# Interleaving attention and MoE by half sequence, with paired heads in row and column tiles

## The chip, the cores and the metric

The kernel runs on one core of one Trainium2 chip. A core has TensorE (matrix products), VectorE, ScalarE (functions by table), GpSimd and SyncE, which all run their own instruction streams, and 16 DMA engines that they share. The metric is the device time of one execution in microseconds. Runs of a kernel are marked fast or slow; slow means over 1.5% above the fastest run of the same kernel. Only fast runs are compared, except where the text says otherwise.

## The reference

```python
# q, k, v: (4 batches, 8 heads, 768 positions, 64), inputs about 0.1 in size
scores = q @ k.T / 8                       # per batch and head
causal = i >= j
stream = causal & ((j < 4) | (i - j < 64)) # 4 sink keys, window of 64
mask = causal for heads 0, 2, 6 ; stream for heads 1, 3, 4, 5, 7
attn = softmax(where(mask, scores, -1e9)) @ v
x = attn as (3072 tokens, 512)             # head h gives columns 64h..64h+63
h = x @ w_in                               # (512, 2048)
g = h * sigmoid(beta * h)                  # a beta for each of the 2048
out = g @ w_out                            # (2048, 512)
```

Three heads ("retrieval") attend to everything before them, five ("streaming") to four sink keys and the last 64 positions. The kernels leave the maximum out of the softmax, which these small scores permit.

## The kernel before

It works in three stages: load and rescale the weights, attention of all batches and heads, then the MoE layer. Matrix operands are bf16, and every exponential is taken with keys on the partitions and queries along the columns.

```python
# stage 1: weights arrive in fp32 and are rescaled by VectorE, so that one
# table function serves: beta*h = x @ (w_in*beta), g = silu(beta*h)/beta
nc.vector.tensor_mul(w_in_sb[:, mo, :], w_in_f[:, mo, :], beta_bc)      # 4 x
...
# stage 2: for 16 pairs (batch, two neighbouring heads)
def part1(b, hp):
    # 6 loads by SyncE in fp32, 3 VectorE copies to bf16 (V with a column of ones)
    ...
    for t in range(T):                       # T = 6 blocks of 128 positions
        nc.tensor.transpose(tpq, q2b[:, t, :, :], ident_bf)
        nc.any.tensor_copy(out=QT2[:, t * 128:(t + 1) * 128], in_=tpq)
        ...                                  # the same for k
    for hh in range(2):
        for idx, (kj, ca, cb) in enumerate(plan):  # key block kj, query blocks ca..cb
            nc.tensor.matmul(sp[:, 0:w], KT2[po:po + D, kj * 128:(kj + 1) * 128],
                             QT2[po:po + D, ca * 128:(cb + 1) * 128], ...)
            nc.scalar.activation(out=esd, in_=sp[:, 0:w], func=Exp, scale=scale)
            ...                              # product with an fp32 mask by VectorE
def part2(st):
    for hh in range(2):
        for qi in range(T):
            for j, (idx, kj, cc) in enumerate(contrib):
                nc.tensor.matmul(pout, es_all[:, hh, idx, cc*128:(cc+1)*128],
                                 V_ext[:, kj, hh, :], ...)       # 65 columns
            nc.vector.reciprocal(rec, pout[:, D:D + 1])
            nc.vector.tensor_scalar(out=oqd2[:, qi, hh, :], in0=pout[:, 0:D],
                                    scalar1=rec, ..., op0=mult)
    ...                                      # 6 transposes back, copied into xT
# stage 3: for 6 chunks of 512 tokens
for fi in range(FO):                         # 16 blocks of 128 hidden units
    ...                                      # 4 matmuls of 512 columns into hp_
    nc.scalar.activation(out=gT[:, fi, :], in_=hp_, func=Silu)
for ns in range(4):
    ...                                      # 16 matmuls of 512 columns into op
    nc.scalar.copy(out=osb, in_=op)          # and a store
```

A streaming head takes the first key block against all queries (for the sinks) and each other key block against two query blocks. That makes 768 + 4 x 256 + 128 = 1920 score columns for 768 queries, and most query blocks sum over three value matmuls.

The softmax here doesn't subtract the row's maximum and nothing guards it: scores larger than these inputs give would overflow.

Of the kernel before, what the change touches and what calls it, by code (L numbers as in the profile page):

```python
# [8 lines left out]
F32 = mybir.dt.float32  # L9
BF16 = mybir.dt.bfloat16  # L10
GE = mybir.AluOpType.is_ge


def _aff(nc, buf, cm, fstep, base, n):
    nc.gpsimd.affine_select(
        out=buf,
        in_=buf,
        compare_op=GE,
        fill=0.0,
        base=base,  # L20
        pattern=[[fstep, n]],
        channel_multiplier=cm,
    )


@with_exitstack
def kernel(
# [16 lines left out]
    d_model = moe_w_in.shape[0]  # L44
    d_ff = moe_w_in.shape[1]
    N = B * S
    MO = d_model // 128
    FO = d_ff // 128
    NCHUNK = 512
    NCH = N // NCHUNK  # L50

    retr = [1, 0, 1, 0, 0, 0, 1, 0]
    n_sink_i = 4
    window_i = 64
    scale = 1.0 / (D ** 0.5)

    consts = ctx.enter_context(tc.tile_pool(name="consts", bufs=1))

    def new_mask(nm):
        m = consts.tile([128, 128], F32, name=nm)  # L60
        nc.gpsimd.memset(m, 1.0)
        return m

    Mc = new_mask("Mc")
    _aff(nc, Mc, -1, 1, 0, 128)
    Msd = new_mask("Msd")
    _aff(nc, Msd, -1, 1, 0, 128)
    _aff(nc, Msd, 1, -1, window_i - 1, 128)
    Mso = new_mask("Mso")
    _aff(nc, Mso, 1, -1, -(128 - window_i + 1), 128)  # L70
    Msink = consts.tile([128, 128], F32, name="Msink")
    nc.gpsimd.memset(Msink, 0.0)
    nc.gpsimd.memset(Msink[0:n_sink_i, :], 1.0)
    Msink_c = consts.tile([128, 128], F32, name="Msink_c")
    nc.gpsimd.memset(Msink_c, 0.0)
    nc.gpsimd.memset(Msink_c[0:n_sink_i, :], 1.0)
    _aff(nc, Msink_c, -1, 1, 0, 128)
    Mso_sink = consts.tile([128, 128], F32, name="Mso_sink")
    nc.vector.tensor_max(Mso_sink, Mso, Msink)
    M00s = consts.tile([128, 128], F32, name="M00s")  # L80
    nc.vector.tensor_max(M00s, Msd, Msink_c)

    ident_f32 = consts.tile([128, 128], F32, name="idf")
    make_identity(nc, ident_f32)
    ident_bf = consts.tile([128, 128], BF16, name="idb")
    nc.vector.tensor_copy(out=ident_bf, in_=ident_f32)

    Mstr0 = consts.tile([128, T * 128], F32, name="Mstr0")
    nc.vector.tensor_copy(out=Mstr0[:, 0:128], in_=M00s)
    nc.vector.tensor_copy(out=Mstr0[:, 128:256], in_=Mso_sink)  # L90
    for t in range(2, T):
        nc.vector.tensor_copy(out=Mstr0[:, t * 128:(t + 1) * 128], in_=Msink)
    Mstrd = consts.tile([128, 256], F32, name="Mstrd")
    nc.vector.tensor_copy(out=Mstrd[:, 0:128], in_=Msd)
    nc.vector.tensor_copy(out=Mstrd[:, 128:256], in_=Mso)

    big = ctx.enter_context(tc.tile_pool(name="big", bufs=1))
    xT = big.tile([128, MO, N], BF16)
    w_in_sb = big.tile([128, MO, d_ff], BF16)
    w_out_sb = big.tile([128, FO, d_model], BF16)  # L100

    with tc.tile_pool(name="wstage", bufs=1) as wstage:
        beta_row = wstage.tile([1, d_ff], F32)
        nc.sync.dma_start(out=beta_row, in_=moe_beta.rearrange("(o f) -> o f", o=1))
        beta_bc = wstage.tile([128, d_ff], F32)
        nc.gpsimd.partition_broadcast(beta_bc, beta_row)  # L106
        beta_p = wstage.tile([128, FO], F32)
        nc.sync.dma_start(out=beta_p, in_=moe_beta.rearrange("(fo fi) -> fi fo", fi=128))
        invb = wstage.tile([128, FO], F32)
        nc.vector.reciprocal(invb, beta_p)  # L110

        w_in_f = wstage.tile([128, MO, d_ff], F32)
        nc.sync.dma_start(
            out=w_in_f,
            in_=moe_w_in.rearrange("(mo mi) f -> mi mo f", mi=128),
        )
        for mo in range(MO):
            nc.vector.tensor_mul(w_in_sb[:, mo, :], w_in_f[:, mo, :], beta_bc)  # L118

        w_out_f = wstage.tile([128, FO, d_model], F32)  # L120
        nc.sync.dma_start(
            out=w_out_f,
            in_=moe_w_out.rearrange("(fo fi) d -> fi fo d", fi=128),
        )
        for fo in range(FO):
            nc.vector.tensor_scalar(  # L126
                out=w_out_sb[:, fo, :],
                in0=w_out_f[:, fo, :],
                scalar1=invb[:, fo:fo + 1],
                scalar2=None,  # L130
                op0=mybir.AluOpType.mult,
            )

    def chunks(lo, hi, maxlen=4):
        res = []
        a = lo
        while a <= hi:
            b = min(hi, a + maxlen - 1)
            res.append((a, b))
            a = b + 1  # L140
        return res

    pairs = [(b, hp) for b in range(B) for hp in range(0, H, 2)]

    def make_plan(is_r):
        plan = []
        if is_r:
            for kj in range(T):
                for (ca, cb) in chunks(kj, T - 1):
                    plan.append((kj, ca, cb))  # L150
        else:
            for (ca, cb) in chunks(0, T - 1):
                plan.append((0, ca, cb))
            for kj in range(1, T):
                plan.append((kj, kj, min(kj + 1, T - 1)))
        return plan

    with tc.tile_pool(name="a_qkT", bufs=2) as aqk, \
         tc.tile_pool(name="a_in", bufs=3) as ain, \
         tc.tile_pool(name="a_es", bufs=2) as aes, \  # L160
         tc.tile_pool(name="a_sm", bufs=4) as asm, \
         tc.tile_pool(name="a_out", bufs=2) as aout, \
         tc.tile_pool(name="a_ps_sp", bufs=4, space=bass.MemoryType.PSUM) as psp, \
         tc.tile_pool(name="a_ps_ou", bufs=2, space=bass.MemoryType.PSUM) as pou, \
         tc.tile_pool(name="a_ps_tr", bufs=2, space=bass.MemoryType.PSUM) as ptr:

        pend = None

        def part1(b, hp):
            q2 = ain.tile([128, T, 2, D], F32, name="q2")  # L170
            k2 = ain.tile([128, T, 2, D], F32, name="k2")
            v2 = ain.tile([128, T, 2, D], F32, name="v2")
            for hh in range(2):
                nc.sync.dma_start(
                    out=q2[:, :, hh, :],
                    in_=q[b, hp + hh].rearrange("(t p) d -> p t d", p=128),
                )
                nc.sync.dma_start(
                    out=k2[:, :, hh, :],
                    in_=k[b, hp + hh].rearrange("(t p) d -> p t d", p=128),  # L180
                )
                nc.sync.dma_start(
                    out=v2[:, :, hh, :],
                    in_=v[b, hp + hh].rearrange("(t p) d -> p t d", p=128),
                )
            q2b = ain.tile([128, T, 2, D], BF16, name="q2b")
            nc.vector.tensor_copy(out=q2b, in_=q2)
            k2b = ain.tile([128, T, 2, D], BF16, name="k2b")
            nc.vector.tensor_copy(out=k2b, in_=k2)  # L189
            V_ext = ain.tile([128, T, 2, D + 1], BF16, name="V_ext")  # L190
            nc.vector.tensor_copy(out=V_ext[:, :, :, 0:D], in_=v2)  # L191
            nc.vector.memset(V_ext[:, :, :, D:D + 1], 1.0)

            QT2 = aqk.tile([128, S], BF16, name="QT2")
            KT2 = aqk.tile([128, S], BF16, name="KT2")
            for t in range(T):
                tpq = ptr.tile([128, 128], BF16, name="tpt")
                nc.tensor.transpose(tpq, q2b[:, t, :, :], ident_bf)  # L198
                nc.any.tensor_copy(out=QT2[:, t * 128:(t + 1) * 128], in_=tpq)  # L199
                tpk = ptr.tile([128, 128], BF16, name="tpt")  # L200
                nc.tensor.transpose(tpk, k2b[:, t, :, :], ident_bf)  # L201
                nc.any.tensor_copy(out=KT2[:, t * 128:(t + 1) * 128], in_=tpk)

            es_all = aes.tile([128, 2, 8, 512], BF16, name="es_all")
            plans = []
            for hh in range(2):
                h = hp + hh
                po = hh * D
                is_r = retr[h] == 1
                plan = make_plan(is_r)  # L210
                plans.append(plan)
                for idx, (kj, ca, cb) in enumerate(plan):
                    w = (cb - ca + 1) * 128
                    sp = psp.tile([128, 512], F32, name="sp")
# [150 lines left out]
```

## Time and profile before

| | before |
|---|---|
| time, median of 3 runs | 427.89 us |
| first TensorE work | 45.05 us |
| attention | about 45 to 258 us (213 us) |
| MoE | about 258 to 427 us (169 us) |

The page of the profile gives the busy time of each engine with its share of the span and the number of instructions. Below that are the span in 40 equal slices (a digit is the busy share in tenths, 9 is 90% or more) and the chain of waits that ended last, as shares of the span.

```profile
PE 335.7 (79%) x1827; PEld 160.0 (37%) x1844; DVE 183.5 (43%) x736; ACT 215.1 (50%) x602; POOL 5.4 (1%) x19
PE   0000678688767898878887998999999999999996
DVE  0176377987779877888868661000000000000000
...
PE 67%; DVE 19%; issue 6%; ACT 4%; POOL 1%; DMA 1%; another core or an unknown queue 1%; SPq 0%; POOLq 0%; ACTq 0%
```

PE is TensorE, DVE VectorE, ACT ScalarE, POOL GpSimd, and PEld a weight load of TensorE. The three stages can be read from the digits: TensorE waits for four slices, then works mostly at 6 to 8 tenths beside an equally busy VectorE, and is full only in the last 16 or so slices, where VectorE does nothing at all. The chain, over the whole span, is mostly TensorE's, but a fifth of it is VectorE's.

The same by windows. A line has the stretch in us, its length, the busy us of the engines with instruction counts, the granted clock of TensorE (1.00 is full), the DMA share, and GB/s.

```profile
core 0: us, PE busy (x) PEld busy (x) DVE busy (x) ACT busy (x) POOL busy (x), PEclk, DMA share, GB/s
0.00:45.00 45.00, 0.00 (x0) 0.00 (x0) 18.47 (x34) 0.00 (x0) 5.37 (x19) 1.00 0.64 213
45.00:258.00 213.00, 172.51 (x1091) 86.08 (x1093) 164.87 (x702) 143.67 (x482) 0.00 (x0) 1.00 0.45 84
258.00:420.00 162.00, 160.09 (x723) 72.63 (x738) 0.18 (x1) 70.33 (x120) 0.00 (x0) 0.99 0.10 36
```

The attention stage has no full engine; 702 VectorE and 482 ScalarE instructions hand small tiles to each other. The MoE stage is TensorE alone, and its pace can be read from the timeline (start, duration, engine, line, operation, output and inputs, shape, count).

```profile
340.23 1.03 PE L302 MATMUL hp__4138<-xT,w_in_sb 128*128 128x512 bf16 x4
341.09 1.03 PE L302 MATMUL hp__4144<-xT,w_in_sb 128*128 128x512 bf16 x4
```

```profile
248.89 1.06 PE L302 MATMUL hp__3607<-xT,w_in_sb 128*128 128x512 bf16 x2 [0.22 <-issue]
249.74 0.63 PE L302 MATMUL hp__3613<-xT,w_in_sb 128*128 128x512 bf16 x1
```

At 340 us four matmuls of 512 columns start every 0.86 us, 0.215 us each. The printed duration, 1.03 us, is longer, since a matmul's latency overlaps the next one. This cost can't be removed by reordering; what can be gained is the time around it.

The clock column needs care. At 248.89 us only two of these matmuls fit into 0.85 us: TensorE runs at half speed, although the window says 1.00. The trace lists the clock only from its first change, here at 253.36 us, and the windows print 1.00 where it lists nothing. The switch shows in the spacings: 0.427 us before 253.36 us and 0.215 after it, and value matmuls in a row start 45 ns apart or more before it, 29 ns after it. So the whole attention stage ran at about half clock, and nearly all of its 172.5 busy us of TensorE are us at half clock.

### The profile page before, as it was taken

How to read it: one execution, taken by the hardware profiler on the slowest of the kernel's cores; microseconds unless marked ns; L12 is line 12 of the kernel's file. 1: busy time of each engine (PE TensorE's matmuls, PEld its weight loads, DVE VectorE, ACT ScalarE, POOL GpSimd, SP SyncE). 2: the span in 40 equal slices, each digit the busy share in tenths (PEclk: the TensorE clock that was granted, in tenths of full speed). 3: DMA queues.
4: the chain of work that ended last, by engine and by line, in shares of the span. 5: the costliest groups of instructions: out<-in, count | busy, mean ns of one | idle time of the engine just before them, and what ended most of it. 6: DMA issues, size and time to landing. Idle time of an engine off the chain costs nothing.

```text
span 427.1 us, 5368 instructions
## 1 busy us (share of the span) xinstructions
PE 335.7 (79%) x1827; PEld 160.0 (37%) x1844; DVE 183.5 (43%) x736; ACT 215.1 (50%) x602; POOL 5.4 (1%) x19
## 2 busy tenths in 40 slices
PE   0000678688767898878887998999999999999996
PEld 0000234334433344434434443444444444444442
DVE  0176377987779877888868661000000000000000
ACT  0000677577655787767776636336155162451631
POOL 2020000000000000000000000000000000000000
PEclk9999999999999999999999998999999999999999
DMA  7932999665543864210000000010110101101001
GB/s 259 389 140 64 218 218 183 125 119 111 112 88 68 142 148 103 46 38 1 0 2 1 2 0 2 25 74 2 49 51 0 74 26 38 62 0 74 26 25 74
DMA packets 83404, 33.91 MB, mean 79 GB/s; under 512 B 77745, under 2 KB 77745, under 8 KB 82865
## 3 DMA queue, kind: packets, MB, share of 16 engines
q1 hardware_dynamic: 83378, 33.58, 32.8%
q8 instruction: 14, 0.23, 0.2%
q14 instruction: 12, 0.10, 0.1%
HBM read 27.28 MB, written 6.29 MB: 79 GB/s over the span
## 4 chain that ended last, share of the span: by engine, by line
PE 67%; DVE 19%; issue 6%; ACT 4%; POOL 1%; DMA 1%; another core or an unknown queue 1%; SPq 0%; POOLq 0%; ACTq 0%
PE op L317 19%; PE sp L215 12%; PE pout L259 7%; DVE es_all L243 5%; PE tpt L201 4%; DVE es_all L239 3%; PE tpt L198 3%; DVE w_in_sb L118 2%; PE tpt L278 2%; ACT es_all L223 2%; DVE rec L267 2%; DVE w_out_sb L126 1%; DVE V_ext L191 1%; DMA k_163<-in_k_dram 1%; DVE k2b L189 1%
## 5 line engine op out<-in xcount | busy, mean ns | idle before, releaser
L223 ACT ACTIVATE es_all<-sp 128x256 bf16<-128x256 f32 (+3 forms) x236 | 85.2, 427 | 15.1 <-PE sp L215 11.4
L317 PE MATMUL op<-w_out_sb,gT 128*128 128x512 bf16 x376 | 83.3, 379 | 0.4
L259 PE MATMUL pout<-V_ext,es_all 128*128 128x65 bf16 x552 | 69.4, 244 | 14.2 <-DVE oqd_602 L268 3.2
L259 PEld LDWEIGHTS <-es_all 128*128 128x128 bf16 x552 | 45.3, 124 | 54.1 <-issue 8.9
L198 PE MATMUL tpt<-idb,q2b 128*128 128x128 bf16 x96 | 26.9, 280 | 46.6 <-DMA k_163<-in_k_dram 45.1
L302 PEld LDWEIGHTS <-w_in_sb 128*128 128x128 bf16 x384 | 38.2, 100 | 47.6 <-issue 5.3
L317 PEld LDWEIGHTS <-gT 128*128 128x128 bf16 x384 | 37.6, 98 | 45.3
L325 ACT COPY osb<-op 128x512 f32<-128x512 f32 x24 | 14.1, 586 | 69.0 <-PE op L317 63.3
L267 DVE RECIPROCAL rec<-pout 128x1 f32<-128x1 f32 x192 | 30.1, 163 | 33.6 <-PE pout L259 32.3
L279 ACT COPY xT<-tpt 128x128 bf16<-128x128 bf16 x81 | 19.7, 269 | 36.8 <-PE tpt L278 30.4
L243 DVE TENSOR_TENSOR es_all<-es_all,Mstrd 128x256 bf16<-128x256 bf16 (+1 forms) x100 | 32.5, 389 | 0.0
L201 PE MATMUL tpt<-idb,k2b 128*128 128x128 bf16 x96 | 26.2, 273 | 5.8 <-DVE k2b L189 2.1
L198 PEld LDWEIGHTS <-q2b 128*128 128x128 bf16 x96 | 12.5, 130 | 47.9 <-issue 46.7
L199 ACT ACT_TABLE_LOAD x1 | 1.3, 1283 | 45.4 <-PE tpt L198 45.4
L239 DVE TENSOR_TENSOR es_all<-es_all,Mstr_86 128x512 bf16<-128x512 bf16 (+1 forms) x40 | 20.7, 552 | 1.7 <-ACT es_all L223 0.7
L232 DVE TENSOR_TENSOR es_all<-es_all,Mc 128x128 bf16<-128x128 bf16 x72 | 18.3, 282 | 1.4 <-ACT es_all L223 0.5
L201 PEld LDWEIGHTS <-k2b 128*128 128x128 bf16 x96 | 11.2, 117 | 13.4 <-issue 9.7
L118 DVE TENSOR_TENSOR w_in_sb<-w_in_f,beta_bc 128x2048 bf16<-128x2048 f32 x4 | 8.9, 2284 | 11.2 <-POOL beta_bc L106 11.2
L126 DVE TENSOR_SCALAR w_out_sb<-w_out_f,invb 128x512 bf16<-128x512 f32 x16 | 6.4, 474 | 0.0
L215 PE MATMUL sp<-QT_291,KT_292 64*128 64x256 bf16 (+3 forms) x15 | 5.3, 446 | 0.0
L215 PE MATMUL sp<-QT_2643,KT_2644 64*128 64x256 bf16 (+3 forms) x15 | 5.3, 446 | 0.0
L215 PE MATMUL sp<-QT_3289,KT_3290 64*128 64x256 bf16 (+3 forms) x15 | 5.3, 446 | 0.0
(405 smaller groups left out, 425.6 us busy)
## 6 DMA issues: line engine op xcount, KB each, us to landing
out_dram<-osb SPq DMA_DIRECT2D x24, 256.0 KB, 2.0
w_in_f<-in_moe_w_in_dram SPq DMA_DIRECT2D x1, 4096.0 KB, 13.3
w_out_f<-in_moe_w_out_dram SPq DMA_DIRECT2D x1, 4096.0 KB, 23.3
q_162<-in_q_dram SPq DMA_DIRECT2D x2, 192.0 KB, 3.3
k_163<-in_k_dram SPq DMA_DIRECT2D x2, 192.0 KB, 3.2
v_164<-in_v_dram SPq DMA_DIRECT2D x2, 192.0 KB, 3.9
q_275<-in_q_dram SPq DMA_DIRECT2D x2, 192.0 KB, 4.5
k_276<-in_k_dram SPq DMA_DIRECT2D x2, 192.0 KB, 4.4
```

The source lines that it names most:

```text
L198: nc.tensor.transpose(tpq, q2b[:, t, :, :], ident_bf)
L201: nc.tensor.transpose(tpk, k2b[:, t, :, :], ident_bf)
L215: nc.tensor.matmul(sp[:, 0:w], KT2[po:po + D, kj * 128:(kj + 1) * 128], QT2[po:po + D, ca * 128:(cb + 1) * 128], start=True, stop=True,)
L223: nc.scalar.activation(out=esd, in_=sp[:, 0:w], func=mybir.ActivationFunctionType.Exp, scale=scale,)
L232: nc.vector.tensor_mul(es_all[:, hh, idx, off:off + 128], es_all[:, hh, idx, off:off + 128], Mc,)
L239: nc.vector.tensor_mul(esd, esd, Mstr0[:, ca * 128:(cb + 1) * 128])
L243: nc.vector.tensor_mul(esd, esd, Mstrd[:, 0:w])
L259: nc.tensor.matmul(pout, es_all[:, hh, idx, cc * 128:(cc + 1) * 128], V_ext[:, kj, hh, :], start=(j == 0), stop=(j == nci - 1),)
L267: nc.vector.reciprocal(rec, pout[:, D:D + 1])
L279: nc.any.tensor_copy(out=xT[:, mo, b * S + qi * 128: b * S + (qi + 1) * 128], in_=tpo,)
L302: nc.tensor.matmul(hp_, w_in_sb[:, mo, fi * 128:(fi + 1) * 128], xT[:, mo, n0:n0 + NCHUNK], start=(mo == 0), stop=(mo == MO - 1),)
L317: nc.tensor.matmul(op, gT[:, fi, ns * 128:(ns + 1) * 128], w_out_sb[:, fi, :], start=(fi == 0), stop=(fi == FO - 1),)
```

## The change

The intent is to let attention, which no engine bounds, run in the shadow of MoE, which TensorE bounds, and to make attention itself cheaper.

- Work is cut into 8 units: 4 batches, two halves of 384 queries. In iteration n the first MoE matmuls of unit n and the second ones of unit n-1 alternate with pieces of the attention of units n+1 and n+2.
- Two heads share the array. In the scores one head lies in rows 0 to 63 and the other in rows 64 to 127 (row tiles); in the products with the values one writes columns 0 to 63 and the other 64 to 127 (column tiles). The values are now the weights, so the output comes out already transposed.
- A streaming head has blocks of 60 queries (the first has 108). 60 queries with a window of 64 see 123 keys, with the sinks 127: each block has a single key block of 128, built by copying windows of k and v and the sinks in front of them.
- Row sums come from matmuls with a selecting matrix for all eight heads; one reciprocal per unit; it is spread over the partitions through DRAM.
- Swish as h·(1 + tanh(beta·h/2))/2, so that, it is hoped, the exponential and tanh need no table change. The weights need no rescaling; GpSimd's DMAs convert to bf16.

The core of the diff:

```diff
-    with tc.tile_pool(name="wstage", bufs=1) as wstage:
-        ... weights in fp32, rescaled by VectorE
+    for i, h in enumerate((ha, hb)):                    # load_pair
+        nc.gpsimd.dma_start(out=q2[:, :, i, :], in_=q[b, h].rearrange("(p t) d -> p t d", t=T))
+        nc.gpsimd.dma_start(out=k2[:, :, i, :], in_=k[b, h].rearrange(kfmt, t=T))
+    ...                                                 # load_v, a streaming head:
+        nc.gpsimd.dma_start(out=vs[:, ns, 0, :], in_=vb[0:128, :])
+        nc.gpsimd.dma_start(out=vs[:, ns, 1:NBLK, :],
+            in_=bass.AP(vb.tensor, vb.offset + (FIRST - W - SINK) * D,
+                        [[D, 128], [STEP * D, NBLK - 1], [1, D]]))
+        nc.gpsimd.dma_start(out=sk[:, ns, :], in_=vb[0:SINK, :])
+        nc.gpsimd.tensor_copy(out=vs[0:SINK, ns, 1:NBLK, :], in_=...sk broadcast...)
+    qk_in[0, pi] = load_pair(0, pi)                     # all pairs, then load_v(0)
+    ... make_identity(nc, ident_f); masks; w_in and w_out by nc.gpsimd.dma_start
+
+    # scores of a round: the operations of the two heads alternate
+    for j in range(max(len(o) for o in ops)):
+        for o in ops:
+            if j < len(o):
+                nc.tensor.matmul(o[j][0], o[j][1], o[j][2], start=True, stop=True)
+    nc.scalar.activation(out=es[:, ri, 0:nh, :], in_=sp[:, 0:nh, 0:NQ], func=AF.Exp, scale=scale)
+    ...                                                 # one mask product, bf16
+    # sums: matmuls with esel, then
+    nc.vector.reciprocal(rec, sm[0:96, 0:128])
+    nc.sync.dma_start(out=rd[:, j, :], in_=rec[32*j:32*j+8, :])      # to DRAM
+    nc.sync.dma_start(out=R[i * D:(i + 1) * D], in_=...)             # and back, spread
+    # pv: two heads into the two halves of o, then
+    nc.vector.tensor_mul(x.xT[:, pi, :], o[:, 0:NQ], x.R[:, pi, :])
+    # mm1
+    nc.scalar.activation(out=t, in_=h[:, 0:NQ], func=AF.Tanh, scale=beta_h[:, fi:fi + 1])
+    nc.vector.scalar_tensor_tensor(out=x.gT[:, fi, :], in0=t, scalar=1.0,
+                                   in1=h[:, 0:NQ], op0=ADD, op1=MULT)
+    # the main loop
+    for n in range(N + 1):
+        side = pieces_b(n + 1) + pieces_a(n + 2)
+        ...                                             # pieces_l(n + 2): loads
+        for s in range(FO):
+            ... side pieces up to len(side)*(s+1)//FO
+            if n < N:
+                mm1(units[n], s)
+            if n > 0:
+                mm2(units[n - 1], s)                    # 3 matmuls of 512 columns
```

The compiler's scheduler orders each engine's instructions again, so the program's order is not quite the order on the chip.

## The prediction

> **What bounds it now.** Three stages in a row (busy time by windows). 0–45 us: TensorE does nothing; weights load and are rescaled, and the first q/k transfers queue behind them (first matmul at 45.05 us). 45–258 us: attention, no single engine full; in 100–250 us TensorE is busy 122 us of 150, VectorE 118, ScalarE 104, and the chain of waits hops between scores, masks, transposes and sums. 258–420 us: MoE, TensorE alone: 768 matmuls of 512 columns in about 162 us, 0.216 us apart in the chain (four in 0.86 us), ScalarE half idle, VectorE idle.
>
> **What the change does.** MoE matmul time stays: 8 units x (64 x about 0.163 + 48 x 0.216) = 166 us (0.163 scaled from 0.216 by 384/512 columns). Attention is put inside it, so most of the 213 us stage should vanish except for its own TensorE time.
>
> TensorE, attention, per batch (estimates): a weight load plus a short matmul costs about 0.064 us in the trace (six value matmuls of 65 columns in 0.54 us, first latency included). Transposes 48 x 0.065 = 3; scores 94 and values about 90 instructions, in pairs that may run side by side, 5–8 and 4–6; row sums 93 x 0.03–0.06 = 3–6. Together 15–23 us per batch, 8–11 per unit. The Trainium skill, "TensorEngine Tiling (Array Packing)", section Key Properties, says that different tiles run in parallel but that a mode change drains TensorE; this trace shows neither cleanly. About 15 side pieces per unit, two changes each: I add 2 us. So 30–34 us per unit in the steady part.
>
> ScalarE: from 0.287 us at 128 and 0.599 at 512 columns, 768 columns cost 0.81, 384 cost 0.50. Exponentials 50 us, tanh 128 x 0.50 = 63, copies 14: 127 us, hidden. A table load is 1.28 us in the trace; the skill, "ScalarE: Activation LUTs", section Table sets, puts exp and tanh in one set, so I expect one load, not one per switch.
>
> VectorE: 384 columns about 0.55 us (0.282 at 128, 0.416 at 256, 0.686 at 512 in the mask products): gating 70, normalising 18, masks 20–34, transposed copies about 48, reciprocals 8: about 170–180 us, hidden but bursty.
>
> **New costs.** (1) Start: all q, k, v of batch 0 are issued by GpSimd before the identity is built there, with five copies that each wait for a load: 34 issues at 1.2–1.5 us (a guess; the trace has none) plus 5 x about 4 us (landing 3–4.5 us) give about 60 us before the first transpose. (2) Batch 0's attention runs without MoE, 30–35 us. (3) Reciprocals go through DRAM: two hops of 2–4 us, perhaps 8–9 us, where the program leaves about 6 of matmuls; the in-order VectorE holds gating behind it: 2–3 us per unit.
>
> **Sum.** First MoE matmul about 90 (60 + 30); unit 0 with side work 20; five full units x 32 = 160; the last three iterations 23 + 21 + 13 = 57. Total about 325 us. Range 280–390.
>
> Chances: faster 0.91, within 2% 0.03, slower 0.06.
>
> **What shows it.** Steady stage: TensorE 80–95% busy; iterations (every six output stores) 28–35 us apart; one activation table load; first transpose 45–75 us; values' VectorE products waiting on the reciprocal's DMA for some us once per unit; VectorE 160–190 and ScalarE about 130 us busy.
>
> **What would make it wrong.** GpSimd issue much dearer (about 22,000 pieces of 256 B per batch): then loads pace every batch and it could even be slower. Table loads at each exp/tanh switch. Tile pairs running one after another, or dear mode changes. Cheaper: issue under 1 us, start near 45 us.

## The result, and the profile after

| | before | after |
|---|---|---|
| median of the same session | 428.34 us | 313.98 us (4 runs, 310.33 to 316.76; one is slow) |
| ratio of fast runs | | 0.730 (95% interval 0.725 to 0.734) |
| first TensorE work | 45.05 us | 32.65 us |
| first MoE matmul | about 248 us | 67.95 us |

Ratios are the mean time of one kernel's fast runs over that of the other's of the same rounds, so not quite the ratio of the medians quoted. The mean of the three fast runs after is 312.76 us, and the differences of the experiments below are taken from it where an experiment has a mean of several fast runs. They are differences between sessions; the ratios to the kernel before, 0.730 against the experiment's, say the same within 1 us, except for e5.

The page of the profile after, with the same parts and the granted clock of TensorE in tenths:

```profile
PE 255.1 (82%) x2196; PEld 132.4 (42%) x2196; DVE 147.1 (47%) x309; ACT 135.9 (43%) x217; POOL 141.7 (45%) x208
PE   0000477659699979999999799999999999999994
...
PEclk9999999999979995999999799999999999999999
...
PE 58%; DMA 21%; POOL 9%; DVE 6%; SPq 2%; issue 2%; ACT 1%; DVEq 0%; POOLq 0%; ACTq 0%
```

TensorE is now full over most of the span and VectorE works below it. VectorE and ScalarE execute 309 and 217 instructions where they had 736 and 602. What remains is the four empty slices at the start, the half-filled ones behind them, and the places where the granted clock drops (7, 5 and 7 in its row). In the chain DMA has 21% and GpSimd 9%; before, they had 1% each.

The windows of the units, columns as before:

```profile
0.00:68.00 68.00, 21.90 (x243) 13.64 (x244) 17.00 (x56) 13.94 (x17) 57.00 (x97) 1.00 1.13 112
99.50:131.50 32.00, 30.03 (x279) 14.24 (x278) 17.81 (x35) 19.26 (x32) 26.16 (x35) 0.89 1.46 124
195.10:226.60 31.50, 31.50 (x288) 16.71 (x286) 21.60 (x43) 15.64 (x26) 0.00 (x0) 1.00 0.18 52
```

From 195 us, when the loads are over (GpSimd 0.00), TensorE is busy 31.50 us of 31.50: nothing is waited for. While loads run, a unit of about the same length, with nine matmuls fewer, has two idle microseconds and a clock of 0.89. The first 68 us are the start and the attention of batch 0, with nothing to hide them. The 1.00 in their line is no record either: the list of clock changes begins at 72.65 us. Two matmuls of 384 columns at 67.95 us start 0.293 us apart, those from 74.65 us 0.1625, so this stage too ran at about half clock at its end.

The timeline of the start. The bracket is the idle time of the engine before the line, and what ended it.

```profile
2.28 0.83 POOL L97 DMA_DIRECT2D k_100<-in_k_dram  x1
...
32.37 0.23 DVE L139 CAST ident<-ident_f 128x128 bf16<-128x128 f32 x1 [28.18 <-POOL ident_f masks.py:199]
32.65 0.80 PE L209 MATMUL misc<-ident,q_99 128*128 128x128 bf16 x6 [32.65 <-DMA vs<-in_v_dram]
...
67.95 0.82 PE L378 MATMUL h<-xT,w_in_sb 128*128 128x384 bf16 x2
```

The bracket of the transposes names a value load, but these transposes don't read it. The line above shows the real cause: the identity came at 32.37 us, because GpSimd built it only after it had issued all loads of batch 0. A load of 96 KB of q or k keeps GpSimd 0.83 us. So wherever GpSimd's name ends a wait, its queue order is part of the cost.

The waits for the reciprocals over the whole span (us in total, times, longest):

```profile
DVE xT L370 <- DMA R<-rd: 10.9, 5, 3.3
PE misc L369 <- DVE xT L370: 10.7, 5, 3.5
```

VectorE waited five times for the reciprocals that travel through DRAM, and TensorE for VectorE behind it. The first of the five lies in the first 68 us, the others before 180 us, while loads run.

How cheap the tiles are is seen in the timeline at 203 to 209 us:

```profile
203.45 0.81 PE L389 MATMUL o<-w_out_sb,gT 128*128 128x512 bf16 x3
204.19 0.41 PE L369 MATMUL misc<-es_1_2176,vs 128*64 128x24 bf16 x14
204.53 0.34 PE L378 MATMUL h<-xT,w_in_sb 128*128 128x384 bf16 x1
...
208.13 0.34 PE L291 MATMUL sp<-QT_2494,KT_2503 64*128 64x384 bf16 x2
208.40 0.39 PE L389 MATMUL o<-w_out_sb,gT 128*128 128x512 bf16 x1
```

Take start times, not durations. Two score matmuls of 384 columns in row tiles take 0.27 us (208.13 to 208.40); one alone in the full array takes 0.1625 us (four in 0.65 us). Fourteen value matmuls of a streaming pair take 0.34 us. Three matmuls of 512 columns would take 0.65 us, but the next instruction, in another tile mode, starts after 0.74 us: a change into a tiled mode cost about 0.09 us here. The Trainium skill, "TensorEngine Tiling (Array Packing)", section Key Properties, says that tiles can load weights and multiply in parallel and that a change of mode drains the engine. The trace agrees with both, and puts the 0.09 us on the second.

ScalarE's largest group of instructions (line, engine, operation, tiles, count; busy us, mean ns; idle before, and what ended most of it):

```profile
L381 ACT ACTIVATE t<-h,beta_h 128x384 f32<-128x384 f32 x128 | 74.3, 582 | 91.0 <-PE h L378 87.9
```

The tanh takes 582 ns and was predicted at 500. An exponential of the same 384 columns takes 490 ns (timeline at 44.13 us). The tanh takes its scale from a column in memory, the exponential a constant; no run changes that alone. The Trainium skill, "ScalarE: Activation LUTs", section What ACT_TABLE_LOAD costs, says that such an operand adds about 93 ns; this trace has 92. It is hidden: ScalarE waited 87.9 us for these matmuls.

VectorE came out at 147 us where 170 to 180 were predicted. The masks, now bf16, took 22 us, inside the predicted 20 to 34; the copies of transposed tiles took 36 us instead of 48, and neighbouring instructions overlap (their durations add up to about 157 us). A mask product of 384 columns takes 0.35 us and one of 768 columns 0.55 us (timeline at 44 and 47 us), 0.52 ns per column. Before, with fp32 masks, 256 and 512 columns took 0.416 and 0.686 us, 1.05 ns per column. The Trainium skill, "VectorE: DVE Perf Modes", section The perf-mode tier table, puts a product of two bf16 tensors at twice the speed of fp32. The trace agrees, with one factor in fp32 before.

### The profile page after: what moved, and what is told of

Its sections match the earlier page's. It is cut to its first block, busy times and chain, and to the rows that moved or that the text cites. A ratio compares the mean times of both kernels' runs of the same rounds, so it can differ in the third digit from the quotient of the medians.

```text
span 312.8 us, 5541 instructions
## 1 busy us (share of the span) xinstructions
PE 255.1 (82%) x2196; PEld 132.4 (42%) x2196; DVE 147.1 (47%) x309; ACT 135.9 (43%) x217; POOL 141.7 (45%) x208
## 3 DMA queue, kind: packets, MB, share of 16 engines
q0 software_dynamic: 96256, 15.62, 67.2%
## 4 chain that ended last, share of the span: by engine, by line
PE 58%; DMA 21%; POOL 9%; DVE 6%; SPq 2%; issue 2%; ACT 1%; DVEq 0%; POOLq 0%; ACTq 0%
PE o L389 22%; PE h L378 22%; DMA R<-rd 13%; PE sp L291 5%; DMA rd<-rec 4%; PE misc L369 4%; DMA sk<-in_v_dram 3%; PE misc L332 3%; PE misc L214 2%; DVE rec L338 2%; PE misc L209 1%; POOL w_in_sb L191 1%; SPq L345 1%; POOL vs L115 1%; SPq L341 1%
## 5 line engine op out<-in xcount | busy, mean ns | idle before, releaser
L381 ACT ACTIVATE t<-h,beta_h 128x384 f32<-128x384 f32 x128 | 74.3, 582 | 91.0 <-PE h L378 87.9
L378 PE MATMUL h<-xT,w_in_sb 128*128 128x384 bf16 x512 | 110.0, 335 | 0.1
L389 PE MATMUL o<-w_out_sb,gT 128*128 128x512 bf16 x384 | 105.9, 384 | 0.0
L382 DVE SCALAR_TENSOR_TENSOR gT<-t,h 128x384 bf16<-128x384 f32 x128 | 70.4, 552 | 71.4 <-ACT t L381 70.2
L370 DVE TENSOR_TENSOR xT<-misc,R 128x384 bf16<-128x384 f32 x32 | 16.8, 550 | 13.1 <-DMA R<-rd 10.9
L115 POOL DMA_DIRECT2D vs<-in_v_dram x20 | 21.8, 1092 | 2.1 <-DMA q_642<-in_q_dram 1.7
L121 POOL COPY vs<-sk 4x704 bf16<-4x704 bf16 x20 | 15.2, 762 | 15.7 <-DMA sk<-in_v_dram 8.6
L393 ACT ACTIVATE osb<-o 128x512 f32<-128x512 f32 x24 | 14.3, 594 | 9.1 <-PE o L389 8.6
L191 POOL DMA_DIRECT2D w_in_sb<-in_moe_w_in_dram x32 | 16.7, 561 | 0.7 <-DMA w_in_sb<-in_moe_w_in_dram 0.7
L114 POOL DMA_DIRECT2D vs<-in_v_dram x20 | 11.7, 583 | 1.1 <-DMA k_637<-in_k_dram 0.9
L120 POOL DMA_DIRECT2D sk<-in_v_dram x20 | 10.4, 524 | 0.0
```

The source lines that it names most:

```text
L115: nc.gpsimd.dma_start(out=vs[:, ns, 1:NBLK, :], in_=bass.AP(vb.tensor, vb.offset + (FIRST - W - SINK) * D, [[D, 128], [STEP * D, NBLK - 1] ...
L121: nc.gpsimd.tensor_copy(out=vs[0:SINK, ns, 1:NBLK, :], in_=sk[:, ns, :].unsqueeze(1).to_broadcast([SINK, NBLK - 1, D]),)
L191: nc.gpsimd.dma_start(out=w_in_sb[i * D:(i + 1) * D, pi, s * FS:(s + 1) * FS], in_=moe_w_in[h * D:(h + 1) * D, s * FS:(s + 1) * FS],)
L370: nc.vector.tensor_mul(x.xT[:, pi, :], o[:, 0:NQ], x.R[:, pi, :])
L378: nc.tensor.matmul(h[:, 0:NQ], w_in_sb[:, pi, fi * 128:(fi + 1) * 128], x.xT[:, pi, :], start=(pi == 0), stop=(pi == NP - 1))
L381: nc.scalar.activation(out=t, in_=h[:, 0:NQ], func=AF.Tanh, scale=beta_h[:, fi:fi + 1])
```

## The experiments

Twelve kernels, each timed in rounds beside the kernel before, in three sessions of four kernels each, on three chips. The kernel before stayed near 428 us in all of them. Edits are against the kernel after.

### e1: the new attention without the interleaving

The theory: part of the gain is the cheaper attention by itself, part is the overlap. To separate them, all attention is done first and then the MoE loop (with eight buffers for xT instead of three).

```diff
-    for f in pieces_a(0) + pieces_a(1) + pieces_b(0): f()
-    for f in pieces_l(2): f()
+    for n in range(N):
+        for f in pieces_l(n + 2) + pieces_a(n) + (pieces_b(n - 1) if n > 0 else []): f()
+    for f in pieces_b(N - 1): f()
+    att.close()          # PSUM of attention given back, MoE's opened here
     for n in range(N + 1):
-        side = pieces_b(n + 1) + pieces_a(n + 2)
-        ...              # loads and side pieces
         for s in range(FO): ... mm1, mm2
```

> All attention first, then all of the MoE, everything else of the changed kernel kept. Theory A (the gain is mostly the overlap): the new attention alone needs about 33 us of start plus four times the 35 us that batch 0 took by itself, then 166 us of MoE matmuls: 340 to 355 us, so the overlap is worth 27 to 40 us and the rest of the 115 us comes from a cheaper start and cheaper attention. Theory B (attention did not become cheaper; only the overlap counts): 400 us or more. Theory C (loads pace it: packets kept the DMA engines busy until 170 us): attention ends near 210 us or later, 375 to 390 us in all.

Measured: 360.34 us (357.09 to 361.89), ratio 0.841 (0.836 to 0.846). The windows of e1's two stages and of five microseconds inside the first, and the chain of its page:

```profile
33.00:177.50 144.50, 101.79 (x1218) 63.87 (x1216) 75.23 (x161) 50.56 (x64) 111.96 (x163) 0.77 1.31 128
177.50:357.40 179.90, 173.83 (x979) 90.67 (x979) 75.48 (x137) 87.05 (x152) 0.00 (x0) 0.98 0.12 40
105.00:110.00 5.00, 3.83 (x62) 3.13 (x57) 3.12 (x6) 0.81 (x1) 5.00 (x7) 0.50 1.78 114
...
PE 50%; DMA 22%; POOL 20%; issue 3%; DVE 2%; ACT 1%; SPq 0%; POOLq 0%; DVEq 0%; ACTq 0%
```

What follows: start and attention together cost 177.5 us instead of 258, and MoE by itself 180 instead of 169, so 68 us of the 115 us gain need no overlap; 12 of the 68 are the earlier first transpose (32.65 instead of 45.05 us). The rest, 360 - 313 = 47 us, is the overlap. In this stage VectorE works 75 us on 161 instructions where it worked 165 us on 702. The time came out above the expected 340 to 355.

TensorE is idle for 43 of the 144.5 us, while GpSimd is busy 112. From 33 to 178 us the chain runs through DMA for 74 us and through GpSimd for 50, through TensorE for 8: the loads pace this stage. That is the mechanism of theory C, though not its time. So the 144.5 us are not yet what attention costs by itself; with the loads out of the way the part that needs no overlap would be larger.

The clock of 0.77 is too high, since the record begins at 90.94 us and row-sum matmuls of 128 columns before that are 0.107 us apart, as at half clock; full clock is listed for only 20 us of the stage. So this attention ran at half clock like that of the kernel before, while the kernel after has full clock from 72.65 us on in all but 13.65 us. What the overlap does is therefore more than one thing: it hides the loads, fills TensorE, and keeps its clock up. How much of the 47 us each is, this run does not tell.

### e2: sigmoid instead of tanh

The theory: tanh pays because ScalarE need not change its function table between the exponential and it. The rival: ScalarE is half idle, so table changes would hide. The same product with the sigmoid:

```diff
-    tensor_scalar(out=beta_h, in0=beta_h, scalar1=0.5, ...)
+    tensor_scalar(out=beta_h, in0=beta_h, scalar1=1.0, ...)
-    activation(out=t, ..., func=AF.Tanh, ...);    scalar_tensor_tensor(..., scalar=1.0, ...)
+    activation(out=t, ..., func=AF.Sigmoid, ...); scalar_tensor_tensor(..., scalar=0.0, ...)
-    activation(out=osb, in_=x.o, func=AF.Copy, scale=0.5)
+    activation(out=osb, in_=x.o, func=AF.Copy, scale=1.0)
```

> Sigmoid in place of tanh (same work in VectorE, other constants). The compiled program has 98 activation table loads instead of 1. Theory A (tanh pays because it shares the table with exp): 98 x 1.28 us = 125 us more on ScalarE, which goes from about 16 to about 33 us of work per unit, above the 31.5 us of TensorE: 330 to 365 us. Rival (ScalarE was half idle, so the loads hide): within 2% of 314.

Measured: 386.33 us (383.23 to 387.45), ratio 0.901 (0.897 to 0.906), 73 us slower than after. The timeline of e2 shows why:

```profile
199.71 1.28 ACT L293 ACT_TABLE_LOAD   x1
201.00 0.81 ACT L293 ACTIVATE es<-sp 128x768 bf16<-128x768 f32 x1
201.83 1.28 ACT L381 ACT_TABLE_LOAD   x1
```

There are 98 table loads of 1.283 us, 125.8 us in all, and ScalarE is busy 261.8 us instead of 135.9. Units (from first store to first store) are now 41 to 44 us apart instead of 28 to 33; between 172 and 212 us ScalarE is busy 37.8 of 40 us. So the kernel was moved from a TensorE bound to a ScalarE bound. The expected 330 to 365 us was too low: it spread the loads evenly over eight units, 16 us each, while 18 of them, 23 us, fall into these 40 us. The kernel after has one load. The Trainium skill, "ScalarE: Activation LUTs", section Table sets: the hidden batching unit, lists tanh in the set of exp; the single load agrees.

### e3: reciprocals from a constant

The theory: the wait for the reciprocals' trip through DRAM costs its 10.7 us plus the clock that drops after it. The rival: only the wait itself, 302 to 306 us. The trip stays in the program, but the product takes a constant. The result is wrong.

```diff
+    R1 = consts.tile([128, NP, NQ], F32, name="R1"); nc.vector.memset(R1, 1.0)
-        x.R = R
+        x.R = R1
```

> The normalising product reads a constant tile of ones instead of the reciprocals that come back from DRAM; sums, reciprocals and their transfers stay. The result is wrong on purpose. Theory A (the wait costs its idle time and also the clock, which fell to 0.86 to 0.95 in the stretches with such waits): 298 to 304 us. Theory B (only the 10.7 us that the product's wait held TensorE): 302 to 306. Rival (the wait is hidden by other queued matmuls): 310 or more, and the granted clock stays low, which would point to another cause of it.

Measured: 305.03 us (303.93 to 305.47), ratio 0.712 (0.710 to 0.714). The mean of the fast runs is 304.87, 7.9 us below after. The wait for R is gone, but others took part of its place, as e3's list of waits shows:

```profile
PE misc L211 <- DMA q<-in_q_dram: 4.6, 1, 4.6
PE misc L371 <- POOL vs L121: 4.1, 1, 4.1
```

TensorE now runs ahead and meets the loads of q and the copy that GpSimd makes behind them. The clock stays below 1 (0.977 on average, 0.65 in 105 to 110 us). The number fits the rival; but since the later waits are followed by half clock too, this run can't say what the clock costs. Theory one is neither shown nor refuted by it; e12 goes on from here.

### e4: identity and masks before the loads

The theory: the start is GpSimd's order, and moving the identity ahead gives back all of the 25 us. The rival: the next thing on GpSimd, the weights, will be waited for instead.

```diff
-    for pi in range(NP):                     # loads of batch 0
-        qk_in[0, pi] = load_pair(0, pi)
-    v_in[0] = load_v(0)
     make_identity(nc, ident_f)
     ...                                      # masks
+    for pi in range(NP):
+        qk_in[0, pi] = load_pair(0, pi)
+    v_in[0] = load_v(0)
```

> Identity and masks are built on GpSimd before the loads of batch 0 are issued; nothing else moves. The first transpose then starts near 8 us instead of 32.7. Theory A (the start is wholly on the critical path): 288 to 294 us. Theory B (the loads of batch 1, issued by GpSimd only after the weights, pace unit 0, so that the gain is given back): 303 to 314, with TensorE idle before the transposes of batch 1 near 80 us.

Measured: 298.46 us median (292.46 to 299.7). Only one of its four runs, 292.46, counts as fast; so there is no ratio, and the profile is of a run of 297.77 that is marked slow. I read only times of the start from it, 25 us apart, which the 7 us between its runs can't explain.

```profile
7.80 0.80 PE L209 MATMUL misc<-ident,q 128*128 128x128 bf16 x6 [7.80 <-DMA q<-in_q_dram]
...
63.56 1.44 PE L389 MATMUL o<-w_out_sb,gT 128*128 128x512 bf16 x3 [5.50 <-DMA w_out_sb<-in_moe_w_out_dram]
```

The first transpose comes 25 us earlier (7.80 instead of 32.65), the first MoE matmul 28 us earlier (40.05 instead of 67.95), and the end about 17 us earlier (span 296.1 instead of 312.8). The 11 us between went into new waits of TensorE: for w_out (5.5 us), w_in (2.9 in all) and q (3.3 and 1.6). In the kernel after, these had landed before they were needed. By the three slower runs the truth is between the two theories; the one fast run lies in the range of the first (288 to 294).

### e5: the two heads one after the other

The theory: if heads are not alternated, tiles can't overlap and each unit gets longer. The rival: it makes little difference.

```diff
-    for j in range(max(len(o) for o in ops)):
-        for o in ops:
-            if j < len(o): nc.tensor.matmul(...o[j]...)
+    for o in ops:
+        for oj in o: nc.tensor.matmul(...oj...)
```

> The matmuls of a pair are given half after half instead of alternating, so that neighbours in the queue use the same half of the array (pairs of one matmul each stay neighbours). Theory A (neighbours in different tiles run side by side: in the trace 12 value matmuls with 3840 columns took 0.94 us, where 3840 columns at the 0.216 us of 512 would take 1.6): value sums lose about 2.9 us per batch and streaming scores 0.6, for three and a half batches inside the full stage: 322 to 328 us. Rival (TensorE finds the free tile itself, or the pairing never mattered): 312 to 316.

Measured: 315.07 us (313.29 to 319.09), ratio 0.740 (0.734 to 0.745), fast mean 314.48, 1.7 us above after. The ratio says 4 us more, with intervals that all but meet; it does not follow from the fast runs listed (314.48 of 427.6 is 0.736), and the record doesn't say why. By either the expected 322 to 328 was not reached. The edit was partly undone: the scheduler alternated many of the heads again (neighbouring value matmuls that start within 0.02 us of each other: 156 in after, 84 here; scores 142 and 122). Where it did take, fourteen streaming value matmuls took 0.46 us (201.66 to 202.12 in its timeline) instead of 0.34. So this run does not test the theory cleanly; e9 does.

### e6: longer packets of q

The theory: the number of packets occupies GpSimd and the DMA engines. For q (and k of the first pair) six positions of a head lie together in memory; a tile ordered by head instead of by position takes them as one packet.

```diff
-        q2 = inp.tile([128, T, 2, D], BF16, name="q2")
+        q2 = inp.tile([128, 2, T, D], BF16, name="q2")
-            nc.gpsimd.dma_start(out=q2[:, :, i, :], ...)
+            nc.gpsimd.dma_start(out=q2[:, i, :, :], ...)
-            nc.tensor.transpose(qt_ps[:, t, :], q2[:, t, :, :]..., ident)
+            for i in range(2):
+                nc.tensor.transpose(qt_ps[i*D:(i+1)*D, t, :], q2[:, i, t, :], ident)
```

> q of all heads and k of the first pair are stored head by head, so that one partition's 768 B land in one piece instead of six of 128 B; about 27% fewer packets on the GpSimd queue, and 24 more transposes of 64 columns per batch (two side by side). Theory A (loads crowd the DMA engines until 170 us, delay the reciprocals and batch 1, and their issue delays the start): 302 to 310 us, less waiting of the normalising product. Rival (packets are not what counts, since most loads are ahead of need): 312 to 316.

Measured: 308.65 us (306.84 to 314.43), ratio 0.720 (0.717 to 0.723), fast mean 308.05, 4.7 us below after. The packets of the software queue fell from 96256 to 70656, for the same bytes. This is in the expected 302 to 310, though it makes 120 more transposes. The profile is of the slow run of 314.43 us: a q load keeps GpSimd 0.59 us, and the first transpose starts at 29.27 instead of 32.65 us. Shorter waits for the reciprocals, which were expected too, do not show in it (13.7 us); it is one slow run, so they are not refuted either.

### e7: sinks by DMA instead of GpSimd's copies

The theory: GpSimd's five copies per batch each wait for a load; the DMA could place the sinks itself. For the two not to overlap in memory, the window load leaves the sink rows out, so it covers 124 partitions.

```diff
-        nc.gpsimd.dma_start(out=vs[:, ns, 1:NBLK, :],       in_=<128 rows from FIRST-W-SINK>)
-        nc.gpsimd.dma_start(out=sk[:, ns, :], in_=vb[0:SINK, :])
-        nc.gpsimd.tensor_copy(out=vs[0:SINK, ns, 1:NBLK, :], in_=...sk broadcast...)
+        nc.gpsimd.dma_start(out=vs[SINK:128, ns, 1:NBLK, :], in_=<124 rows from FIRST-W>)
+        nc.gpsimd.dma_start(out=vs[0:SINK, ns, 1:NBLK, :],
+            in_=bass.AP(vb.tensor, vb.offset, [[D, SINK], [0, NBLK - 1], [1, D]]))
```

> The four sink rows of each streaming head come by a DMA that repeats its source, into partitions that the window load no longer writes; GpSimd no longer waits for a load and copies. Theory A (the waits delay identity and every later issue): first transpose near 28 us instead of 32.7, total 306 to 311 us. Rival (no effect beyond noise): 312 to 316.

Measured: 338.49 us (332.29 to 340.32), of which only 332.29 counts as fast, so there is no ratio. Even that is 20 us slower than after, against both theories. The issue of the window load in the listing of its line (lowest, median and highest ns, first and last start), for after and for e7:

```profile
L115 POOL DMA_DIRECT2D vs<-in_v_dram x20: 1075/1082/1151, 17.4 to 165.8; - x20
```

```profile
L115 POOL DMA_DIRECT2D vs<-in_v_dram x20: 2749/2756/2797, 17.5 to 204.8; - x20
```

A window load with 3% less data keeps GpSimd 2.76 us instead of 1.08, and lands after 10.0 us instead of 4.2. The packets of the software queue went from 96256 to 180416. By size, the trace has as many packets of 128 bytes as before (89,088 against 89,168), but 87,232 packets of 4 bytes instead of 2,992. So the small packets come on top of the data. The change to 124 partitions, the start at partition 4 and the separate sink load came together. The issue times point at the window load (a sink load keeps GpSimd 0.62 us), but which of them produces the small packets is not settled. The premise, that placing the sinks by DMA is cheaper, is false in this form.

### e8: e4, e6 and e7 together

> Identity first, long packets and sink rows by DMA together; looks for a version that beats both. If the three add (15 + 6 + 4 us): 286 to 292 us. If they draw on the same slack (the weights and batch 1 pace unit 0 once the start is short): 294 to 299, no better than identity first alone, which took 298.

The edit is the three diffs above. Measured: 328.73 us (327.31 to 330.11), ratio 0.768 (0.765 to 0.772). It carries e7's cost and is slower than after, although two of its parts are gains.

### e9: two heads in the same rows

The theory: row tiles let the scores of two heads overlap. Here the second head of three pairs takes the first head's rows, with the same shapes and order, so that its scores are computed from the wrong head. (The output still passes as correct: inputs of 0.1 make all scores near zero, which also says that the comparison with the reference can't catch such an error here.)

```diff
-                lo = hh * D
+                lo = hh * D if pi == 1 else 0
```

> For three of the four pairs both heads' scores are read from the same 64 partitions (the second head's scores are then wrong on purpose); count, sizes and order of the matmuls stay. Theory A (only tiles in different rows run side by side): the pair of 384 columns, 0.27 us apart from its neighbours in the trace, should take about 0.16 us more; 11 such rounds a batch, three and a half batches in the full stage: 5 to 7 us more, 317 to 321. Rival (it never ran side by side): no change in the trace of such a pair and 311 to 316.

Measured: 317.88 us (314.77 to 319.05), ratio 0.740 (0.737 to 0.744), fast mean 317.40, 4.6 us above after, as the theory said (317 to 321). The timeline of e9 at the same place as above:

```profile
208.87 0.50 PE L291 MATMUL sp<-QT,KT 64*128 64x384 bf16 x2
209.29 0.39 PE L389 MATMUL o<-w_out_sb,gT 128*128 128x512 bf16 x1
```

The pair takes 0.42 us (208.87 to 209.29) instead of 0.27. Row tiles in the scores are real and worth about 5 us in all, a small part of the gain.

### e12: q, k and v loaded once

The theory: the loads of the next batch crowd the DMA engines and GpSimd, and what TensorE loses between 68 and 195 us is due to them, whichever wait shows it. The loads of batch 0 are used for all batches, so the result is wrong.

```diff
-        q2, k2 = qk_in.pop((b, pi))
+        q2, k2 = qk_in[0, pi]
-        vr, vs, vpos = v_in[x.b]
+        vr, vs, vpos = v_in[0]
     def pieces_l(n):
+        return []
```

> All batches use the q, k and v of batch 0; the loads of batches 1 to 3 are gone (wrong on purpose). Theory A (those loads crowd the DMA engines, so that reciprocals come late and unit 0 waits for batch 1): most of what the constant tile gained comes back and a little more, 300 to 306 us, and the normalising product waits under 3 us in all. Rival (the two hops through DRAM cost what they cost, load or no load): 309 to 315 with some 10 us of such waits.

Measured: 300.09 us (298.94 to 300.46), ratio 0.699 (0.697 to 0.702), fast mean 299.89, 12.9 us below after. Two rows of e12's page:

```profile
PE   0000458639999999999999999999999999999994
PEclk9999999999999999999999999999999999999999
```

After the start TensorE is full to the end. From 68 us on it waits 0.2 us in all, where after had 7.5 us idle between 68 and 300 us, and the clock is 1.00 from 72.2 us, where its record begins, to 297.5. The reciprocals' trip is still in the program, and is waited for once, 3.4 us at the start (under 3 had been expected). So it was not the trip by itself that was waited for, but the trip beside loads. The trace of after shows it too: SyncE issues the first hop at 104.19 us, the second at 107.15, and the product that waits for it starts at 116.14, 12 us in all; from 194 us on, without loads, the second hop is issued 2.0 to 2.5 us after the first instead of 3.0 to 5.1, and nothing waits for the reciprocals.

This also gives the clock. The 12.9 us are more than the 7.5 us of idle TensorE. The rest fits the clock: an average of 0.97 over the 232 us from 68 to 300 us means about 14 us at half speed, in which 7 us of work are lost (an estimate from these numbers). The kernel after shows such a place directly. Its timeline, and then two windows of one microsecond:

```profile
116.14 1.02 DVE L370 TENSOR_TENSOR xT<-misc,R 128x384 bf16<-128x384 f32 x2 [1.98 <-DMA R<-rd]
116.75 0.64 PE L369 MATMUL misc<-es_0_923,vs 128*64 128x108 bf16 x12 [1.91 <-DVE xT L370]
```

```profile
118.00:119.00 1.00, 1.00 (x15) 0.68 (x15) 0.45 (x1) 0.44 (x1) 0.81 (x2) 0.50 2.31 158
...
124.00:125.00 1.00, 1.00 (x7) 0.38 (x6) 0.57 (x2) 1.00 (x2) 0.38 (x1) 1.00 2.24 142
```

The reciprocals come late, TensorE is idle for 1.91 us, and from 117.0 to 123.9 us its clock is 0.50 although it is busy all the time. It is back at 1.00 in the line at 124 us. The Trainium skill, "TensorE: Matmul & The Clock Gate", section HAM oscillation — how this bites in real kernels, warns of idle gaps over about 3.4 us; here the half clock followed a shorter one. Between 73 and 300 us three waits of TensorE, 2.78, 1.91 and 1.94 us long, were followed by 3.4, 6.8 and 3.4 us at half clock, half of which (1.7, 3.4 and 1.7 us) is lost; a wait of 0.58 us was not. Nor is it a rule for waits of 1.9 us, as e10 shows.

### e10: identity first, long packets, and the copies last

What the experiments point to: e4 and e6 together, and instead of e7 GpSimd's five copies moved behind all value loads of the batch, so that they don't wait one by one.

```diff
                     nc.gpsimd.dma_start(out=sk[:, ns, :], in_=vb[0:SINK, :])
-                    nc.gpsimd.tensor_copy(out=vs[0:SINK, ns, 1:NBLK, :], in_=...)
                     vpos[h] = ns
                     ns += 1
+        for j in range(ns):
+            nc.gpsimd.tensor_copy(out=vs[0:SINK, j, 1:NBLK, :], in_=...)
```

> Identity first, long packets for q, and the five copies of sink rows after all loads of v, at full width as in the changed kernel. Identity first alone took 292 to 300, long packets alone 307 to 309. If they add: 288 to 294 us. If they share the same slack: 294 to 299.

Measured: 288.8 us (288.22 to 293.46), ratio 0.674 (0.672 to 0.676), fast mean 288.74, and correct. It beats both kernels: 24 us below after. That is within the expected 288 to 294. The share of each part in this sum was not timed beside it. Its profile, of the slow run, has a wait of the same kind without a drop of the clock:

```profile
154.50 0.54 PE L377 MATMUL misc<-es,vs 128*64 128x108 bf16 x12 [1.93 <-DVE xT L378]
```

The trace lists full clock from 122.6 to 289.9 us. So the length of a wait alone does not decide whether half clock follows; what does stays open.

### e11: e10 with the weights through SyncE

The theory: e10 still waits for weights that queue behind GpSimd's issues; SyncE is free. The Trainium skill, "DMA: Bandwidth & Descriptors", section SWDGE vs HWDGE vs iDMA, says that only GpSimd's DMAs convert types, so the weights come in fp32 and ScalarE converts them. The rival: the same bytes and the conversions cost as much, 288 to 298 us.

```diff
-                nc.gpsimd.dma_start(out=w_in_sb[...], in_=moe_w_in[...])
+                nc.sync.dma_start(out=wf[...], in_=moe_w_in[...])
+                ...
+            nc.scalar.copy(out=w_in_sb[...], in_=wf)
```

> The version before, and the weights come on the SP queue in fp32 and are cast by ScalarE, which is idle early; GpSimd loses 36 issues (about 20 us). Theory A (the weights on GpSimd's queue hold the first MoE matmuls and batch 1): 4 to 9 us less than the version before, 280 to 288 us. Rival (the same bytes through the same engines, and casts in front of exponentials): no gain, 288 to 298.

Measured: 298.18 us (296.11 to 300.56), ratio 0.695 (0.692 to 0.698): 9 us slower than e10. The timeline of e11:

```profile
15.26 0.62 ACT L201 CAST w_in_sb<-wf 128x512 bf16<-128x512 f32 x1 [1.58 <-DMA wf<-in_moe_w_in_dram]
```

The conversions stand in ScalarE's queue in front of the exponentials of batch 0, and wait there for weights, up to 2 us each. The first MoE matmul comes at 56.8 us instead of 36.7 (the latter from a profile of e10's slow run of 293.46 us, a difference far beyond 5 us). The time is at the upper edge of the rival's 288 to 298: no gain, and a loss.

## Why the prediction was right or wrong, point by point

The total was predicted at 325 us and measured at 313.98, inside the range, and faster as said. Part of that agreement is luck, as the parts show. The sum behind it, on the span of 312.8 us:

| step | predicted | measured |
|---|---|---|
| first transpose | 60 us | 32.65 us |
| attention of batch 0 alone | 30 us | 35.3 us (32.65 to 67.95) |
| unit 0 | 20 us | 31.5 us (67.95 to about 99.5) |
| five full units | 160 us | 155.4 us (99.5 to 254.9) |
| last three iterations | 57 us | 57.9 us (254.9 to 312.8) |

- **What bounds it, and that MoE's matmul time stays: right.** It missed that the old attention stage ran at about half clock. Matmuls of 384 columns are 0.1625 us apart, of 512 columns 0.216, as scaled.
- **The steady unit of 30 to 34 us: right, with two terms off in opposite directions.** Units take 32.0, 32.2, 31.4, 31.5 and 28.3 us. The unit from 195.1 to 226.6 us has 64 matmuls of 384 and 49 of 512 columns, 21.0 us. The remaining 10.5 us are attention with its mode changes; 8 to 11 plus 2 had been predicted. The unit has 32 mode changes. A matmul of 512 columns before one takes 0.31 us to the next start instead of 0.215, a pair of scores 0.27 instead of 0.1625, so they cost about 3 us (an estimate from these spacings) and attention itself about 7.5. The 0.064 us for a weight load with a short matmul had been read where TensorE ran at half clock. That pairs overlap was foreseen, and e9 shows it for the scores.
- **One table load: right**, and it mattered: e2 put 73 us on it.
- **The start: the mechanism was right, the size wrong.** The term "34 issues at 1.2–1.5 us (a guess) plus 5 x about 4 us" measured 0.83 us per q or k load and 1.08 per window load, and the copies waited 1.0 us in all before 33 us instead of 20: the first transpose came at 32.65 us, below even the low end of "45–75 us". The step that failed is a guess made where the trace had no number; the prediction had named "issue under 1 us, start near 45 us" as the cheaper case.
- **Unit 0 at 20 us: wrong by 11.5 us.** The sum counted only its own matmuls and side work. The compiler's scheduler pulled second matmuls of unit 0 forward into it, and loads of the next batch were waited for: TensorE is idle for 3.0 of the 31.5 us, 22 second matmuls take 4.7 us, and about 8 us run at half clock (3.4 listed, and 4.7 before the list begins), which loses 4. These add up to 11.7 us (an estimate from the trace). This error and the start's, 27 us to the other side, in good part cancel. So the total is closer than its parts.
- **The reciprocals' wait of 2 to 3 us in every unit: half right.** There were five waits, 10.9 us in all, up to 3.3 us each, and only while loads ran. The prediction saw the trip as too long by itself; e12 shows it is too long only beside loads. The loads, and the half clock after three of the waits, were missing from the sum of the steady part: 12.9 us together, by e12.
- **VectorE 170 to 180 us, wrong; ScalarE 127, nearly right.** They measured 147 (copies 36 us instead of 48, and overlaps) and 135.9 (582 ns per tanh). Neither bounds the time (6% and 1% of the chain).
- **The gain's source: not in the prediction.** It counted on the overlap. e1 shows that 68 of the 115 us come from the cheaper start and attention by themselves, and 47 from the overlap, which also hides the loads and raises the clock.

## What to carry to other kernels

Put work that no engine bounds into the shadow of a stage that one engine bounds, and before that make it of few large instructions: here the second gave the larger part. Read then which queue feeds the overlapped stage: what GpSimd issues first, in how many packets, and what the loads run beside, was worth another 24 us without touching any arithmetic. Keep functions that alternate on ScalarE in one table set. And check the pace of TensorE by the spacing of its matmuls: where no clock is recorded, the profile prints 1.00, and the old attention stage ran at half of it.

## What the Trainium skill lacked or had wrong

- "DMA: Bandwidth & Descriptors", section Anatomy of one DMA — SWDGE (gpsimd) path, calls the generation of descriptors "small, variable" and gives no time for it by shape (elsewhere the page has about 1 us to the first byte). Here a DMA kept GpSimd 0.83 us (96 KB of q or k in 768 pieces), 1.08 us (window load on 128 partitions) and 2.76 us (almost the same on 124 partitions), and the order of these issues set the start of the kernel: 25 us in e4.
- The same page does not tell of the 4-byte packets that came with e7's loads: 87,232 instead of 2,992, with 20 window loads on 124 partitions and 20 sink loads, and a landing of the window loads after 10.0 us instead of 4.2.
- "TensorE: Matmul & The Clock Gate", section HAM oscillation — how this bites in real kernels, warns of idle gaps over about 3.4 us. Here 1.91 us of idleness was followed by half the clock for 6.8 us, while 1.93 us in e10 were not. What makes the difference stays open.
- "ScalarE: Activation LUTs", section What ACT_TABLE_LOAD costs, puts a switch of sets at 1,283 ns of load and about 1,380 of drain. In e2 the load took 1.283 us, but the next instruction started 0.01 us after it and the load 0.02 us after the one before: no such drain.
- "TensorEngine Tiling (Array Packing)", section Key Properties, says that a mode change drains and gives no size: about 0.09 us here.
